# Loading every fourth K of an attention block by transposing DMAs instead of transposing it on TensorE

## The chip, the cores and the metric

The kernel runs on one core of a Trainium2 chip. The metric is the device time of one execution in microseconds (us). A macro step, the unit in which the kernel's work is counted below, takes a few of them.

Names of the engines: PE is TensorE (PEld its weight loads), DVE VectorE, ACT ScalarE, POOL GpSimd, SP SyncE, whose queue issues the loads.

## What is computed

Two attention blocks, A and B, of the same shape are computed one after the other, and their results are put side by side. In each there are 16 batches, 32 heads, 64 queries, 512 cached keys and a head size of 128; all data are bf16.

```python
B, Sq, D = 16, 64, 640
H, Sk, Dh = 32, 512, 128
q = (x @ wq).reshape(B, Sq, H, Dh).transpose(0, 2, 1, 3)
scores = jnp.einsum("bhqd,bhkd->bhqk", q, k_cache) * (Dh ** -0.5)
p = softmax(scores, axis=-1)
o = jnp.einsum("bhqk,bhkd->bhqd", p, v_cache)
out = o.transpose(0, 2, 1, 3).reshape(B, Sq, H * Dh) @ wo
```

K and V are the bulk: 2 blocks x 16 x 32 x 512 x 128 elements of each, 268 MB together, each read once.

## The kernel before

**Tiling.** A step is one head of a pair of batches, whose 64 queries each fill the 128 partitions. Two steps (two heads) are a macro step m; there are 256. Eight macro steps are a group (16 heads of a pair of batches). Eight groups (all 16 batches) are a pass, for one half of a block's heads; there are four passes. The sums of the first half stay in `outp`, and the second half's are added to them.

**One macro step** goes through these operations, each named by two letters or three in the code:

- KX (PE, L433): 8 transposes of 128 x 128 blocks of K into one PSUM bank, for batch j = 0 and again for j = 1. KE (DVE, L442) evicts each to `ktp_ring`.
- QP2 (PE, L451): the projection of q; QE2 (ACT, L459) evicts it to `qT_ring`.
- SM2 (PE, L467): the scores, four matmuls of 512 columns, into one PSUM bank for each head.
- MX (DVE, L476) finds the row maxima, EX (ACT, L482) makes the exponentials and their sums, RC2 (DVE, L488) the reciprocals, NM (POOL, L496) scales each head's rows from `p_ring` into `pn_ring`.
- TR2 (PE, L505): 8 transposes of the scaled rows; TE2 (DVE, L512) evicts them to `pT_ring`.
- PV2 (PE, L524): the product with V; OE2 (ACT, L532) evicts it.
- OP2 (PE, L540 and L545): the product with wo, summed in PSUM over the group. At its end OVP (ACT) or OVF (DVE, L560) takes the sum out, and after OVF a store sends it away.
- For each group XT (PE, L604) and XE (ACT, L612) transpose the next x.

**Order.** The order on each engine is fixed by hand: a template lists the operations of one slot with the offset of the macro step that each belongs to. Engines run their lists in order and wait for each other by semaphores.

```python
PE_T = (("TR2", 1), ("QP2", 4), ("KX", 4, 0), ("SM2", 3), ("PV2", 1), ("XT", 0), ("OP2", 0), ("KX", 4, 1))
ACT_T = (("QE2", 4), ("OE2", 1), ("XE", 0), ("EX", 3, 0), ("EX", 3, 1), ("OV", 0), ("ST", -1))
DVE_T = (("TE2", 1), ("RC2", 2), ("KE", 4, 0), ("MX", 3, 0), ("MX", 3, 1), ("KE", 4, 1), ("OVF", 0))
POOL_T = (("NM", 0, 0), ("NM", 0, 1))
```

In slot k, PE thus transposes the scaled rows of macro step k+1, transposes K for k+4 and makes the scores of k+3. POOL has NM alone, in order.

**Loads.** K and V come in chunks of four heads, 512 KB for each batch, into rings of `NKB` = 5 and `NVB` = 5 chunks. K is laid out so that partition p holds 8 keys of one head in one run of 2,048 bytes (`(p t) d`, t = 8), V so that it holds 4 keys in runs of 1,024 bytes. After KX and KE, the scores' columns therefore stand in another order of the keys, and NM puts them into the order that V has. wq and wo are loaded in quarters of a pass, two passes deep. All loads go through SP's queue, in one order that a planner makes out of the slot in which each is needed, the slot in which its buffer is free, and a table of durations (`DMA_NS`, for 8 heads of a batch in the case of K and V, against `SLOT_NS` = 3600 for a slot). An issue whose buffer isn't free stops all that stand behind it.

Of the kernel before, what the change touches and what calls it, by code (L numbers as in the profile page):

```python
# [14 lines left out]
class Cfg:  # L15
    G = 4
    HH = 16
    NKB = 5
    NVB = 5
    NX = 2  # L20
# [14 lines left out]
    SLOT_NS = 3600.0  # L35
    DMA_NS = dict(LDK=3100.0, LDV=3100.0, LDWQ=3900.0, LDWO=4300.0, LDX=700.0)


class Op:
# [3 lines left out]
    def __init__(self, eng, kind, idx, reads=(), writes=(), dur=0.0, ts=None, aux=None):  # L43
        self.eng = eng
        self.kind = kind
        self.idx = idx
        self.reads = tuple(reads)
        self.writes = tuple(writes)
        self.sem = None
        self.count = None  # L50
        self.deps = []
        self.waits = []
        self.dur = dur
        self.ts = ts
        self.aux = aux
        self.dma = kind in ("LDK", "LDV", "LDX", "LDWQ", "LDWO", "ST")

# [7 lines left out]
def build_plan(dims, cfg):  # L65
# [19 lines left out]
    def step_info(g):  # L85
        grp = g // SPB
        return grp // NBP, grp % NBP, grp, g % SPB
# [7 lines left out]
    for t in cfg.PE_T:  # L95
        OFF.setdefault(t[0], t[1])

    def make_op(kind, m, sub):
        g0, g1 = 2 * m, 2 * m + 1
        ps_, bp, grp, h0 = step_info(g0)  # L100
        c = g0 // G
# [28 lines left out]
        if kind == "SM2":  # L130
            return mk("pe", "SM2", m, [("qT", m % cfg.NQ), ("ktp", m % cfg.NKT, 0), ("ktp", m % cfg.NKT, 1)],
                      [("SB", 0), ("SB", 1)], "SM2", m)
# [80 lines left out]
    def chunk_pieces(c):  # L213
# [5 lines left out]
        return [(0, 0, 0, G), (0, 1, 0, G)]  # L219

    for c in range(NCHUNK):
        m0 = MPC * c
        for kind, ring, n_ring, cons, tb in (("LDK", "kn", cfg.NKB, "KX", 2), ("LDV", "v", cfg.NVB, "PV2", 2.5)):
            ready = NEG if c < n_ring else MPC * (c - n_ring + 1) - 1 - OFF[cons]
            for pi, (piece, j, hlo, hhi) in enumerate(chunk_pieces(c)):
                op = mk("sp", kind, (c, j, piece), [], [(ring, c % n_ring, gi) for gi in range(hlo, hhi)], kind,
                        m0, aux=(c, j, hlo, hhi, piece), dur=cfg.DMA_NS[kind] * (hhi - hlo) / 8.0)
                loads.append((ready, m0 - OFF[cons] + 0.01 * hlo, tb + 0.001 * pi, op))
# [14 lines left out]

    def sem_key(op):
        if op.kind in ("LDK", "LDV"):
            return ("d_" + op.kind[2:].lower(), op.writes[0][1], op.aux[4])
        if op.kind == "LDX":
            return ("d_x", op.writes[0][1])
        if op.kind in ("LDWQ", "LDWO"):
            return ("d_" + op.kind[2:].lower(), op.aux[0] % 2, op.aux[1])  # L250
        if op.kind == "ST":
            return ("d_out", op.aux % 2)
        if op.kind in ("INIT1", "INIT2"):
            return ("s_init",)
        return ("s_" + op.kind.lower(),)
# [91 lines left out]
def mha_kernel(nc, blocks, out, cfg=None):  # L347
# [17 lines left out]
    HH = SPB  # L365
    NKB, NVB, NX, NXN, NQ, NKT, NP, NPN, NT, NO, NR = (cfg.NKB, cfg.NVB, cfg.NX, cfg.NXN, cfg.NQ, cfg.NKT, cfg.NP,
                                                       cfg.NPN, cfg.NT, cfg.NO, cfg.NR)
# [10 lines left out]
    with contextlib.ExitStack() as es:  # L378
        block = es.enter_context(nc.Block())

        def sb(name, shape, dt):
            return es.enter_context(nc.sbuf_tensor(name, shape, dt))
# [6 lines left out]
        kn_ring = sb("kn_ring", [128, NKB, 2, G // 2, 8, DH], BF16)  # L389
        v_ring = sb("v_ring", [128, NVB, 2, G, 4, DH], BF16)  # L390
        ktp_ring = sb("ktp_ring", [128, NKT, 2, 2, SK], BF16)
        qT_ring = sb("qT_ring", [128, NQ, 2, 128], BF16)
# [64 lines left out]
        def em_QE2(e, op):  # L457
            m = op.idx
            ins = e.activation(qT_ring[:, m % NQ].rearrange("p s q -> p (s q)"), q_ps, ACTF.Copy, scale=scale)  # L459
            return ins, ins  # L460

        def em_SM2(e, op):
            m = op.idx
            first = last = None
            for sub in range(2):
                for j in range(2):
                    ins = e.matmul(s_bank(sub)[64 * j:64 * j + 64, :], qT_ring[:, m % NQ, sub, 64 * j:64 * j + 64],  # L467
                                   ktp_ring[:, m % NKT, sub, j, :], start=True, stop=True, tile_position=(0, 64 * j))
                    first = first or ins
                    last = ins  # L470
            return first, last
# [19 lines left out]
        def em_NM(e, op):  # L491
            g = op.idx
            r = g % NR
            src = p_ring[:, g % NP, :].rearrange("q (th tl pp) -> q th tl pp", th=2, tl=4)
            dst = pn_ring[:, g % NPN, :].rearrange("q (tl pp th) -> q th tl pp", tl=4, th=2)
            ins = e.tensor_scalar(dst, src, recip[:, r:r + 1], 1.0, ALU.mult, ALU.mult)  # L496
            return ins, ins
# [112 lines left out]
        def em_XE(e, op):  # L610
# [3 lines left out]
            return ins, ins  # L614

        def em_LDKV(e, op):
            c, j, hlo, hhi, _piece = op.aux
# [5 lines left out]
            else:  # L623
# [7 lines left out]
                        OVP=em_OVP, OVF=em_OVF, ST=em_ST, XT=em_XT, XE=em_XE, INIT1=em_INIT1, INIT2=em_INIT2,  # L631
                        LDWQ=em_LDWQ, LDWO=em_LDWO, LDX=em_LDX, LDK=em_LDKV, LDV=em_LDKV)

# [86 lines left out]
```

## Time and profile before

| | |
|---|---|
| median of 3 runs | 959.31 us (958.41 to 959.53) |
| profiled execution, span | 956.8 us; no other time of it is on the page |
| PE busy | 919.4 us, 96% of the span |
| DVE busy | 841.9 us, 88% |
| ACT, POOL busy | 567.1 us (59%), 416.9 us (44%) |
| granted TensorE clock | 0.998 |
| moved by DMA | 299.5 MB, mean 313 GB/s |
| KX, L433 | 4,096 matmuls, 314.6 us busy |
| KE, L442 | 512 copies, 353.7 us busy |
| NM, L496 | 512 operations of 843 ns |

The span reaches from the first to the last instruction of the core. Busy times of matmuls overlap, since they are pipelined: eight transposes are 0.61 us long in the timeline while the next group starts 0.45 us after them. What PE spends on a group is better read from start to start.

In a line of a timeline stand the start in us from the span's start, the length, the engine, the line of the kernel, the operation, what it writes and reads, the shapes, the count of merged instructions and, in brackets, how long the engine sat idle before and who ended that. In a line of waits stand who waited for whom, the total in us, how often, and the longest.

### The profile page before, as it was taken

To read this page: it belongs to the slowest core of one execution; us is meant where nothing else is said; L and a number is where in the kernel's file an instruction comes from. 1 tells how busy PE (TensorE), PEld (TensorE's weight loads), DVE (VectorE), ACT (ScalarE), POOL (GpSimd) and SP (SyncE) were. 2 spreads that over 40 slices of the span, in tenths; PEclk is the share of its full clock that TensorE was granted. 3 is DMA by queue.
4 is the path that set the end of the run, shared out by engine and by line. 5 is a ranking of instruction groups with operands and counts; after the bars stand their busy time and mean duration, and the time that the engine had idled before them with its cause. 6 is when DMAs were issued, how large, how long until landed. Compare 5 with 4: busy or idle time off the path is not lost.

```text
span 956.8 us, 34351 instructions
## 1 busy us (share of the span) xinstructions
PE 919.4 (96%) x14755; PEld 733.5 (77%) x15008; DVE 841.9 (88%) x1552; ACT 567.1 (59%) x1585; POOL 416.9 (44%) x518
## 2 busy tenths in 40 slices
PE   4999999999999999999999999999999999999997
PEld 3877777778777777877777787777877778777775
DVE  2898899898899999899999899889899998999996
ACT  1666656666665565656566666666666656565654
POOL 0444444444444444444444444444444444444443
PEclk9999999999999999999999999999999999999999
DMA  9999999999999999888999999988888988899830
GB/s 315 364 365 364 351 365 367 365 368 351 338 337 337 343 330 315 299 292 305 322 332 352 326 353 327 306 294 296 302 305 288 308 301 297 295 297 314 295 124 15
DMA packets 230871, 299.51 MB, mean 313 GB/s; under 512 B 9536, under 2 KB 165184, under 8 KB 230720
## 3 DMA queue, kind: packets, MB, share of 16 engines
q1 hardware_dynamic: 228416, 294.69, 91.0%
q8 instruction: 118, 1.93, 0.8%
q10 hardware_dynamic: 2304, 2.62, 0.8%
q14 instruction: 33, 0.27, 0.1%
HBM read 294.65 MB, written 2.62 MB: 311 GB/s over the span
## 4 chain that ended last, share of the span: by engine, by line
PE 89%; DVE 4%; POOL 3%; issue 2%; SPq 1%; DMA 1%; POOLq 0%; DVEq 0%
PE ps L433 22%; PE ps L524 14%; PE ps L451 14%; PE ps L467 14%; PE ps L505 12%; PE ps L545 7%; PE ps L540 5%; POOL pn_ring L496 3%; DVE out_sb L560 1%; DVE ktp_ring L442 1%; DVE pT_ring L512 1%; PE ps L604 1%; DMA xn_ring<-in_A_x_dram 1%; SPq L626 1%; SPq L583 1%
## 5 line engine op out<-in xcount | busy, mean ns | idle before, releaser
L496 POOL TENSOR_SCALAR pn_ring<-p_ring,recip 128x512 bf16<-128x512 bf16 x512 | 416.3, 843 | 532.7 <-DVE recip L488 532.7
L442 DVE COPY ktp_ring<-ps 128x1024 bf16<-128x1024 bf16 x512 | 353.7, 691 | 105.3 <-PE ps L433 85.1
L482 ACT ACTIVATE p_ring<-ps,negmax 128x512 bf16<-128x512 f32 x512 | 345.6, 684 | 4.8 <-DVE negmax L476 4.8
L476 DVE TENSOR_REDUCE negmax<-ps 128x1 f32<-128x512 f32 x512 | 327.3, 681 | 0.4 <-PE ps L467 0.3
L433 PE MATMUL ps<-ident,kn_ring 128*128 128x128 bf16 x4096 | 314.6, 220 | 2.8 <-DMA kn_ring<-in_A_k_cache_dram 1.6
L532 ACT ACTIVATE oT_ring<-ps 128x256 bf16<-128x256 f32 x256 | 98.0, 383 | 306.0 <-PE ps L524 306.0
L433 PEld LDWEIGHTS ps<-ident,kn_ring 128*128 128x128 bf16 x4096 | 251.9, 98 | 34.2 <-DVE ktp_ring L442 2.6
L524 PEld LDWEIGHTS ps<-pT_ring,v_ring 128*128 128x128 bf16 x4096 | 133.5, 98 | 109.2 <-issue 100.0
L451 PE MATMUL ps<-xT_ring,wq_sb 128*128 128x128 bf16 x2560 | 186.4, 220 | 3.2 <-DMA wq_sb<-in_A_wq_dram 3.2
L512 DVE COPY pT_ring<-ps 128x1024 bf16<-128x1024 bf16 x256 | 174.5, 682 | 4.6 <-PE ps L505 3.8
L524 PE MATMUL ps<-pT_ring,v_ring 128*128 128x64 bf16 x4096 | 163.8, 194 | 3.3 <-issue 1.7
L467 PE MATMUL ps<-ktp_ring,qT_ring 128*64 128x512 bf16 x1024 | 159.8, 392 | 0.4 <-ACT p_ring L482 0.4
L505 PE MATMUL ps<-ident,pn_ring 128*128 128x128 bf16 x2048 | 156.7, 219 | 3.5 <-POOL pn_ring L496 3.5
L451 PEld LDWEIGHTS ps<-xT_ring,wq_sb 128*128 128x128 bf16 x2560 | 155.2, 98 | 3.5 <-DMA wq_sb<-in_A_wq_dram 3.5
L459 ACT ACTIVATE qT_ring<-ps 128x256 bf16<-128x256 f32 x256 | 98.4, 384 | 66.8 <-PE ps L451 66.8
L505 PEld LDWEIGHTS ps<-ident,pn_ring 128*128 128x128 bf16 x2048 | 124.1, 98 | 7.0 <-POOL pn_ring L496 6.7
L545 PE MATMUL ps<-wo_sb,oT_ring 128*128 128x128 bf16 x512 | 112.1, 219 | 13.4
L482 ACT ACTIVATION_READ_ACCUMULATOR p_ring<-ps,negmax 128x1 f32 x512 | 105.0, 205 | 0.0
L540 PE MATMUL ps<-wo_sb,oT_ring 128*128 128x512 bf16 x259 | 97.8, 379 | 0.0
L540 PEld LDWEIGHTS ps<-wo_sb,oT_ring 128*128 128x128 bf16 x512 | 50.1, 98 | 30.6 <-ACT oT_ring L532 0.3
L467 PEld LDWEIGHTS ps<-ktp_ring,qT_ring 128*64 128x64 bf16 x1024 | 36.1, 108 | 27.1 <-ACT p_ring L482 0.6
L545 PEld LDWEIGHTS ps<-wo_sb,oT_ring 128*128 128x128 bf16 x512 | 50.1, 98 | 0.0
(13 smaller groups left out, 112.7 us busy)
## 6 DMA issues: line engine op xcount, KB each, us to landing
kn_ring<-in_A_k_cache_dram SPq DMA_DIRECT2D x128, 512.0 KB, 7.0
v_ring<-in_A_v_cache_dram SPq DMA_DIRECT2D x128, 512.0 KB, 7.2
kn_ring<-in_B_k_cache_dram SPq DMA_DIRECT2D x126, 512.0 KB, 4.8
v_ring<-in_B_v_cache_dram SPq DMA_DIRECT2D x126, 512.0 KB, 5.7
wq_sb<-in_A_wq_dram SPq DMA_DIRECT2D x8, 640.0 KB, 10.4
wo_sb<-in_A_wo_dram SPq DMA_DIRECT2D x8, 640.0 KB, 10.2
wq_sb<-in_B_wq_dram SPq DMA_DIRECT2D x8, 640.0 KB, 8.4
wo_sb<-in_B_wo_dram SPq DMA_DIRECT2D x8, 640.0 KB, 7.5
```

Of the source, the lines that this page charges most:

```text
L433: ins = e.transpose(kt_ps[:, t8, :], kn_ring[:, c % NKB, j, hp, t8, :], ident[:, :])
L442: ins = e.tensor_copy(dst, src)
L451: ins = e.matmul(q_ps[:, sub * 128:(sub + 1) * 128], wq_sb[:, ps_ % 2, kt, hh * DH:(hh + 1) * DH], xT_ring[:, grp % NX, kt, :], start=(kt ...
L467: ins = e.matmul(s_bank(sub)[64 * j:64 * j + 64, :], qT_ring[:, m % NQ, sub, 64 * j:64 * j + 64], ktp_ring[:, m % NKT, sub, j, :], start=T ...
L476: ins = e.reduce_max(negmax[:, r:r + 1], s_bank(g % 2), axis=AX.X, negate=True)
L482: ins = e.activation(p_ring[:, g % NP, :], s_bank(g % 2), ACTF.Exp, bias=negmax[:, r:r + 1], scale=1.0, accum_out=rowsum[:, r:r + 1])
L496: ins = e.tensor_scalar(dst, src, recip[:, r:r + 1], 1.0, ALU.mult, ALU.mult)
L505: ins = e.transpose(pt_ps[:, sub, t, :], pn_ring[:, g % NPN, t * 128:(t + 1) * 128], ident[:, :])
L512: ins = e.tensor_copy(pT_ring[:, m % NT].rearrange("p s t q -> p (s t q)"), pt_ps_flat)
L524: ins = e.matmul(o_ps[:, col:col + 64], v_ring[:, c % NVB, j, gi, t, :], pT_ring[:, m % NT, sub, t, 64 * j:64 * j + 64], start=(t == 0), s ...
L540: ins = e.matmul(out_ps0, oT_ring[:, m % NO, sub, :], wo_sb[:, ps_ % 2, hh, 0:N0], start=(hh == 0), stop=(hh == SPB - 1))
L545: last = e.matmul(out_ps1, oT_ring[:, m % NO, sub, :], wo_sb[:, ps_ % 2, hh, N0:DN], start=(hh == 0), stop=(hh == SPB - 1))
```

## The change

In every macro step with m % 4 == 3 (`DEVERY` = 4), K is loaded by two DMAs, one for each batch, that transpose on their way (`LDKT`). Their source is the 2 x 512 rows of two heads, 256 bytes each, in natural key order; their destination is a new ring `kd_ring` of `NKD` = 2 macro steps, from which SM2 reads. These macro steps have no KX and no KE. The plain K load of a chunk that ends in such a macro step is shortened by two heads. NM of these macro steps reads with a step of four elements and writes densely, to go from the natural key order to that of V. `NKB` goes from 5 to 4, and the planner's table gets a duration for the new loads.

```diff
-    NKB = 5
+    NKB = 4
+    NKD = 2
+    DEVERY = 4
...
-    DMA_NS = dict(LDK=3100.0, LDV=3100.0, LDWQ=3900.0, LDWO=4300.0, LDX=700.0)
+    DMA_NS = dict(LDK=3100.0, LDKT=2200.0, LDV=3100.0, LDWQ=3900.0, LDWO=4300.0, LDX=700.0)
...
+    def by_dma(m):
+        return m % cfg.DEVERY == cfg.DEVERY - 1
+
     def make_op(kind, m, sub):
         g0, g1 = 2 * m, 2 * m + 1
+        if kind in ("KX", "KE") and by_dma(m):
+            return None
...
+    for m in range(NMAC):
+        if by_dma(m):
+            i = m // cfg.DEVERY
+            ready = NEG if i < cfg.NKD else m - cfg.NKD * cfg.DEVERY - OFF["SM2"]
+            for j in range(2):
+                op = mk("sp", "LDKT", (m, j), [], [("kd", i % cfg.NKD)], "LDK", m, aux=(m, j), dur=cfg.DMA_NS["LDKT"])
+                loads.append((ready, m - OFF["SM2"] - 1.5, 2 + 0.001 * j, op))
...
+                if kind == "LDK":
+                    while hhi > hlo and by_dma((c * G + hhi) // 2 - 1):
+                        hhi -= 2
+                    if hhi == hlo:
+                        continue
...
+        kd_ring = sb("kd_ring", [128, NKD, 2, 2, SK], BF16)
...
                     ins = e.matmul(s_bank(sub)[64 * j:64 * j + 64, :], qT_ring[:, m % NQ, sub, 64 * j:64 * j + 64],
-                                   ktp_ring[:, m % NKT, sub, j, :], start=True, stop=True, tile_position=(0, 64 * j))
+                                   (kd_ring[:, (m // cfg.DEVERY) % NKD, j, sub, :] if by_dma(m)
+                                    else ktp_ring[:, m % NKT, sub, j, :]), start=True, stop=True, tile_position=(0, 64 * j))
...
             src = p_ring[:, g % NP, :].rearrange("q (th tl pp) -> q th tl pp", th=2, tl=4)
             dst = pn_ring[:, g % NPN, :].rearrange("q (tl pp th) -> q th tl pp", tl=4, th=2)
+            if by_dma(g // 2):
+                src = p_ring[:, g % NP, :].rearrange("q (p t) -> q t p", t=4)
+                dst = pn_ring[:, g % NPN, :].rearrange("q (t p) -> q t p", t=4)
...
+        def em_LDKT(e, op):
+            m, j = op.aux
+            blk, bp, grp, ps_, hh0 = step_info(2 * m)
+            h0 = (ps_ % NHALF) * HH + hh0
+            src = blocks[blk][1][2 * bp + j, h0:h0 + 2].rearrange("h s d -> (h s) d")
+            ins = e.dma_start_transpose(kd_ring[:, (m // cfg.DEVERY) % NKD, j, :, :].rearrange("p h s -> p (h s)"), src)
+            return ins, ins
```

More of the change, by code (lines that the diff above doesn't have):

```diff
@@ L55, in __init__ @@
         self.aux = aux
-        self.dma = kind in ("LDK", "LDV", "LDX", "LDWQ", "LDWO", "ST")
+        self.dma = kind in ("LDK", "LDKT", "LDV", "LDX", "LDWQ", "LDWO", "ST")
 STAGES = ("LDW", "LDX", "LDK", "LDV", "KX0", "KE0", "KX1", "KE1", "QP2", "QE2", "SM2", "MX0", "MX1", "EX0", "EX1",
@@ L130, in make_op @@
         if kind == "SM2":
-            return mk("pe", "SM2", m, [("qT", m % cfg.NQ), ("ktp", m % cfg.NKT, 0), ("ktp", m % cfg.NKT, 1)],
+            kt = [("kd", (m // cfg.DEVERY) % cfg.NKD)] if by_dma(m) else [("ktp", m % cfg.NKT, 0),
+                                                                         ("ktp", m % cfg.NKT, 1)]
+            return mk("pe", "SM2", m, [("qT", m % cfg.NQ)] + kt,
                       [("SB", 0), ("SB", 1)], "SM2", m)
@@ L244, in sem_key @@
     def sem_key(op):
+        if op.kind == "LDKT":
+            return ("d_kd", op.writes[0][1])
         if op.kind in ("LDK", "LDV"):
@@ L365, in mha_kernel @@
     HH = SPB
-    NKB, NVB, NX, NXN, NQ, NKT, NP, NPN, NT, NO, NR = (cfg.NKB, cfg.NVB, cfg.NX, cfg.NXN, cfg.NQ, cfg.NKT, cfg.NP,
+    NKB, NKD, NVB, NX, NXN, NQ, NKT, NP, NPN, NT, NO, NR = (cfg.NKB, cfg.NKD, cfg.NVB, cfg.NX, cfg.NXN, cfg.NQ, cfg.NKT, cfg.NP,
                                                        cfg.NPN, cfg.NT, cfg.NO, cfg.NR)
@@ L460, in em_QE2, with by_dma @@
             return ins, ins
+        def by_dma(m):
+            return m % cfg.DEVERY == cfg.DEVERY - 1
         def em_SM2(e, op):
@@ L631, in mha_kernel @@
                         OVP=em_OVP, OVF=em_OVF, ST=em_ST, XT=em_XT, XE=em_XE, INIT1=em_INIT1, INIT2=em_INIT2,
-                        LDWQ=em_LDWQ, LDWO=em_LDWO, LDX=em_LDX, LDK=em_LDKV, LDV=em_LDKV)
+                        LDWQ=em_LDWQ, LDWO=em_LDWO, LDX=em_LDX, LDK=em_LDKV, LDKT=em_LDKT, LDV=em_LDKV)
         def run_program(e, prog, final_waits=()):
```

## The prediction

> **What bounds the kernel now.** The page first, for which engine is full. The columns of part 1 are busy time, share of the span and number of instructions; part 2 cuts the span in 40 slices (tenths busy, then GB/s).
>
> ```profile
> PE 919.4 (96%) x14755; PEld 733.5 (77%) x15008; DVE 841.9 (88%) x1552; ACT 567.1 (59%) x1585; POOL 416.9 (44%) x518
> ...
> DMA  9999999999999999888999999988888988899830
> GB/s 315 364 365 364 351 365 367 365 368 351 338 337 337 343 330 315 299 292 305 322 332 352 326 353 327 306 294 296 302 305 288 308 301 297 295 297 314 295 124 15
> ```
>
> PE is full, but so nearly are the DMA engines. For the first nine slices they move about 364 GB/s; later the rate falls to 290 to 305. The queue of SP tells why:
>
> ```profile
> SPq L626 <- PE ps L433: 353.5, 119, 4.0
> SPq L622 <- PE ps L524: 123.4, 81, 2.6
> ```
>
> SP stood 477 us (of 956.8) waiting until PE had freed a K or V buffer. So the late rate is the demand of PE, and 364 GB/s is what the loads reach when nothing holds them.
>
> Then one macro step of the steady part, from the timeline (start, us, engine, line):
>
> ```profile
> 801.05 0.61 PE L505 MATMUL ps<-ident,pn_ring 128*128 128x128 bf16 x8
> 801.26 0.69 DVE L442 COPY ktp_ring<-ps 128x1024 bf16<-128x1024 bf16 x1 [0.23 <-PE ps L433]
> 801.86 0.68 DVE L512 COPY pT_ring<-ps 128x1024 bf16<-128x1024 bf16 x1
> 802.06 0.61 PE L433 MATMUL ps<-ident,kn_ring 128*128 128x128 bf16 x8
> 802.46 0.15 DVE L488 RECIPROCAL recip<-rowsum 128x2 f32<-128x2 f32 x1
> 802.60 0.62 PE L467 MATMUL ps<-ktp_ring,qT_ring 128*64 128x512 bf16 x4
> 802.71 1.63 POOL L496 TENSOR_SCALAR pn_ring<-p_ring,recip 128x512 bf16<-128x512 bf16 x2 [1.95 <-DVE recip L488]
> 804.17 0.61 PE L433 MATMUL ps<-ident,kn_ring 128*128 128x128 bf16 x8
> 804.62 0.55 PE L505 MATMUL ps<-ident,pn_ring 128*128 128x128 bf16 x7
> ```
>
> The reader is to see two loops that close in the same slot. PE's own work runs from TR2 (L505) at 801.05 to the next TR2 at 804.62: 3.57 us with no gap. Beside it runs a chain: TR2, then on DVE the second K eviction (L442), TE2 (L512), RC2 (L488), on POOL the two NM (L496) until 804.34, then the next TR2. It has only 0.28 us to spare. Where OVF (L560) is put into DVE's part of it, it does set the end:
>
> ```profile
> 812.03 0.61 PE L505 MATMUL ps<-ident,pn_ring 128*128 128x128 bf16 x8
> ...
> 812.85 0.81 DVE L560 TENSOR_TENSOR out_sb<-ps,outp 128x640 bf16<-128x640 f32 x1
> ...
> 814.42 1.62 POOL L496 TENSOR_SCALAR pn_ring<-p_ring,recip 128x512 bf16<-128x512 bf16 x2 [2.68 <-DVE recip L488]
> ...
> 816.10 0.62 PE L505 MATMUL ps<-ident,pn_ring 128*128 128x128 bf16 x8 [0.15 <-POOL pn_ring L496]
> ```
>
> NM ends at 816.04 and TR2 starts at 816.10, so the hop is 0.06 us; this slot lasts 4.07 us.
>
> **What the change takes from the compute engines.** 64 of 256 macro steps (m = 3, 7, ...) lose both KX and both KE. By the starts on PE the first KX takes 0.54 us (802.06 to 802.60) and the second 0.45 (804.17 to 804.62): 0.99 us, 63 us in all. DVE loses 2 x 0.69 us in the same slot, 88 us in all. But these all leave one slot, k = m - 4, and the other three keep their 3.57 us. In the shortened slot PE needs 2.58 us, while the chain still stands: the K eviction at its head belongs to the slot before. TR2 to NM's end 3.29 us, plus the hop, 3.35. So PE waits about 0.77 us for NM, and the slot gains 3.57 - 3.35 = 0.22 us: 14 us for 64. The following slot gains nothing, being bound by PE.
>
> One more gain: OVF falls at k = 7, 15, ..., which are slots that lose their KX. There it can run while PE waits for NM, and the slot after starts without the K eviction. The 0.50 us that it costs 16 times (4.07 - 3.57) go: 8 us. The compute engines thus ask for 956.8 - 22 = 935 us of span.
>
> NM of these macro steps reads its source with a step of 4 elements and writes densely, where it now reads densely and writes with a step of 2 (0.843 us each). Nothing shows the new form; from half to double the time gives two-sided bounds of -0.8 and +1.7 us a macro step against a cover of 0.28, so at worst 64 x 1.4 = 90 us on the 935, and no gain if shorter, because those slots are bound by PE. I take no change, the same 512 elements on the same engine being the only row. The Trainium skill (GPSIMD Engine Reference, section on performance pitfalls for Q7 kernels) puts a step in price, about half as much again, where step times element size exceeds 8 bytes; here it is exactly 8, so it would say no change, and this trace shows no such case.
>
> The K ring goes from 5 chunks to 4. A load is then ready 7 macro steps ahead of its KX, 25 us, where the longest K load took 11.0 us to land: nothing. Smaller K loads and an SM2 that reads kd_ring cost nothing on PE, the shapes being the same.
>
> **What it puts on the DMA engines.** This decides. Before: 294.65 MB read and 2.62 written. 64 x 2 loads of 262,144 bytes, 33.6 MB, leave the plain ones: 263.7 MB in all, at 364 GB/s 724 us. What loads at the start fell short by (315 against 364 over 23.9 us) adds 3 us. Behind the last load some work remains; the last KX started at 943.8 of 956.8, and with V landing after K I take 10 of those 13 us. So if the transfers bind, span = 737 + 128 T, with T the time in which the sixteen engines pass one transposing load of 256 KB. It equals 956.8 at T = 1.72 us, and 935 at T = 1.55.
>
> T is not in the trace. Its packets give the bounds. The records have a median of 84 ns for 2,048 bytes, 46 for 1,024, 9 for the 4-byte counts at the end of a load.
> - Below: as now, 8 packets of 2,048 bytes for each engine: 0.67 us. The same bytes are moved, so no less.
> - If only the reading side counts: 84 and 46 ns lie on 8 ns plus 38 for each KB, so a row of 256 bytes takes 17.5 ns; 1,024 rows on 16 engines are 64 each, 1.12 us.
> - Above: each source row is 128 elements that go to 128 partitions. If it is written in 32-byte pieces at 8 + 1.2 ns, 64 x 8 pieces take 4.7 us.
>
> The middle of 1.12 and 4.7 in ratio is 2.3 us. The planner table that is in the diff has 2.2 us. Its other entries stand close to this trace (1.55 us for 512 KB of K, where 364 GB/s gives 1.44), so scaled alike it gives 2.05. I take 2.05, which lies between the two packet rows and a little under their middle. Then 737 + 128 x 2.05 = 999 us of span, and every slot waits for loads, so the 22 us of compute gain are not seen. The end of the program outside the span was 2.5 us (median 959.31 against this execution's 956.8; the page has no other time for it): 1002 us.
>
> The Trainium skill speaks both ways. DMA: Bandwidth & Descriptors, section on latency and other measured facts, has a transposing load at 261 GB/s, which makes an estimated T of 1.0 us and a span of 935. VectorE: DVE Perf Modes, section on the three transpose paths, has 1309 ns for one 128 x 128 block by DMA; eight of them in a row would be an estimated 10.5 us and a span near 2080. No run here shows either.
>
> SP issues 10 loads of K and V in four macro steps, two of them transposing, and waits in order. A load's issue took 0.37 us when free, up to 3.1 when the queue was full. Two at 3.1 and eight at 0.5 are 10 us of 14: hidden. What is behind a transposing load on SP's queue and in the rings (plain K, V, weights) comes later by T, and that is in the sum.
>
> **The rivals.**
> - *Faster, transfers hidden.* T under 1.55 us, as the 17.5 ns row would have it. For it: it is the nearest packet row, and SP's 477 us of waiting are room. Span 935, with some 2 us lost at the start where transfers are short: 937 to 940 with the 2.5.
> - *PE takes the whole gain.* 956.8 - 63 = 894, reported 896. Against it: the 0.28 us of slack of the NM chain, and the slots with OVF that wait for it already. 2 in 100.
> - *Much slower.* The writing side prices the row in small pieces: T = 4.7 makes 737 + 602 = 1339 us. It begins, for this count, at T = 2.6 (1070).
> - *Between.* T from 1.68 to 1.75: transfers just balance what the compute engines gain, about 959.
>
> **How the numbers follow.** A change below about 0.2% can't be told from none here. Forecast (T from 1.75 to 2.6, 963 to 1073 us) 0.43; transfers hidden or nearly (T under 1.68) 0.37 and whole gain 0.02: faster 0.39; between: same 0.04; much slower 0.14. So slower is 0.57. The range for 8 in 10 takes the hidden case, the balance and the forecast, 934 to 1073, and leaves out 0.14 above and 0.03 below. The forecast's own range is 963 to 1073.
>
> **What would show it.** Right: SP's waits for PE at L626 and L622 nearly gone; DMA at 9 in all slices; PE waiting at L433, L467 or L524 for kn_ring, kd_ring or v_ring; T, as the time added for 128 loads beyond 737 us, near 2. In any case L433 shows 3,072 matmuls and L442 384 copies. Wrong: SP still waits for hundreds of us, PE's idle time stands before L505 and is released by pn_ring, some 0.8 us in every fourth slot, and the slots with OVF are 3.57 us long: then T was under 1.55 and the chain through NM sets the time.

## The result and the profile after

The changed kernel takes 1013.34 us, the median of 4 runs (1005.94 to 1014.99), against 958.86 us (957.75 to 959.53, 4 runs) for the kernel before on the same chip. The ratio is 1.0555, with a 95% interval from 1.0519 to 1.0591: slower by 5.6%. The profiled execution took 1014.99 us; its span is 1013.2 us, and the granted TensorE clock in it was 0.983, against 0.998 before. In the changed kernel KX is L458, KE L467, SM2 L495, RC2 L517, NM L528, TR2 L537, PV2 L556 and OVF L592; the K loads are issued at L666, the V loads at L662, the transposing loads at L653.

From the page: the busy times, the DMA rows of the 40 slices, and the packet count.

```profile
PE 905.0 (89%) x13984; PEld 682.4 (67%) x13984; DVE 768.5 (76%) x1424; ACT 565.5 (56%) x1585; POOL 404.9 (40%) x518
...
DMA  9999999999999999999999999999999999999996
GB/s 289 308 285 286 306 284 288 296 318 282 317 309 288 300 296 311 287 304 291 305 322 300 313 305 279 274 320 287 297 319 279 319 292 318 303 290 289 313 306 145
DMA packets 349615, 299.40 MB, mean 295 GB/s; under 512 B 144672, under 2 KB 300320, under 8 KB 349472
```

No compute engine is at its limit any more: PE falls from 96% of the span to 89%, DVE from 88% to 76%. The DMA engines are full to the last slice. Yet they move less than before: the first nine slices, most of them at about 364 GB/s before, are at 284 to 318, and no slice reaches more than 322. Packets under 512 bytes are 144,672 where they were 9,536; 131,072 of them are the 256-byte packets of the transposing loads.

From the waits (who waited for whom, total us, times, longest), the lines of PE in which a load or NM is waited for:

```profile
PE ps L537 <- POOL pn_ring L528: 18.8, 48, 0.6
PE ps L458 <- DMA kn_ring<-in_B_k_cache_dram: 17.5, 19, 2.8
PE ps L458 <- DMA kn_ring<-in_A_k_cache_dram: 17.4, 19, 4.6
PE ps L556 <- DMA v_ring<-in_B_v_cache_dram: 14.3, 12, 3.1
PE ps L556 <- DMA v_ring<-in_A_v_cache_dram: 13.8, 10, 3.9
```

PE now stands for K and V, 63 us in these four lines; with the smaller lines of x, wq and wo it is 78 us, where the kernel before had 12 (x, wq and the first K). The list has no wait for `kd_ring` itself: PE waits for the plain loads that are queued around the transposing ones. This is 65 us more than before, out of the 78 us between the span and the 935 us that the compute engines ask for; what share of the other 13 the lower clock has is not told apart.

The queue of SP, its waits and then a stretch of its timeline (start, us, engine, line, operation, tiles, number of issues merged):

```profile
SPq L653 <- PE ps L495: 124.4, 52, 5.3
SPq L666 <- PE ps L458: 53.0, 57, 2.5
```

```profile
644.58 2.48 SPq L666 DMA_DIRECT2D kn_ring<-in_B_k_cache_dram  x2
647.11 8.00 SPq L653 DMA_TRANSPOSE kd_ring<-in_B_k_cache_dram  x2
655.16 2.85 SPq L662 DMA_DIRECT2D v_ring<-in_B_v_cache_dram  x2
658.05 1.04 SPq L666 DMA_DIRECT2D kn_ring<-in_B_k_cache_dram  x2
```

The list of waits has 177 us of the 477. The timeline says that even this is too much: each issue begins some 0.05 us after the one before it has ended. Added up over the trace, SP is in the middle of an issue for 963 of 1013 us, and only 2 us lie in pauses above 0.1 us. Before, it was 412 us, and the pauses were 489. (Issues don't count as busy, so the view can name PE for time that was spent issuing. Below, "pauses" are counted in this way.) SP no longer waits for buffers. It is held inside its own issues, the longest being the two transposing ones with 8 us.

Last, one shortened slot, from the timeline of PE and POOL:

```profile
603.86 0.61 PE L537 MATMUL ps<-ident,pn_ring 128*128 128x128 bf16 x8
...
605.51 1.62 POOL L528 TENSOR_SCALAR pn_ring<-p_ring,recip 128x512 bf16<-128x512 bf16 x2 [1.94 <-DVE recip L517]
...
607.19 0.62 PE L537 MATMUL ps<-ident,pn_ring 128*128 128x128 bf16 x8 [0.50 <-POOL pn_ring L528]
```

TR2 to TR2 is 3.33 us, and what PE waits for is NM. The predicted slot was 3.35 us. The slot that follows it, with KX in it again, should last 3.57 us; over the run it has a mean of 4.41 and a median of 4.12. The shortened slots keep a median of 3.34, so the waits for loads fall behind each pair of transposing loads and not in every slot.

### The profile page after: what moved, and what is told of

Same layout as the page of the kernel before. It is cut to its first block, busy times and chain, and to the rows that moved or that the text cites. A ratio compares the mean times of both kernels' runs of the same rounds, so it can differ in the third digit from the quotient of the medians.

```text
span 1013.2 us, 32630 instructions
## 1 busy us (share of the span) xinstructions
PE 905.0 (89%) x13984; PEld 682.4 (67%) x13984; DVE 768.5 (76%) x1424; ACT 565.5 (56%) x1585; POOL 404.9 (40%) x518
## 2 busy tenths in 40 slices
DMA packets 349615, 299.40 MB, mean 295 GB/s; under 512 B 144672, under 2 KB 300320, under 8 KB 349472
## 3 DMA queue, kind: packets, MB, share of 16 engines
HBM read 261.10 MB, written 2.62 MB: 260 GB/s over the span
## 4 chain that ended last, share of the span: by engine, by line
PE 44%; DMA 28%; SPq 18%; POOL 4%; DVE 3%; ACT 2%; issue 1%; POOLq 0%; DVEq 0%
DMA kn_ring<-in_B_k_cache_dram 12%; SPq L653 12%; PE ps L458 11%; DMA kn_ring<-in_A_k_cache_dram 11%; PE ps L495 8%; PE ps L556 7%; PE ps L476 6%; PE ps L572 5%; PE ps L537 5%; POOL pn_ring L528 4%; SPq L662 3%; SPq L666 2%; DVE ktp_ring L467 2%; DVE pT_ring L544 1%; PE ps L577 1%
## 5 line engine op out<-in xcount | busy, mean ns | idle before, releaser
L528 POOL TENSOR_SCALAR pn_ring<-p_ring,recip 128x512 bf16<-128x512 bf16 x512 | 404.2, 815 | 601.1 <-DVE recip L517 601.1
L467 DVE COPY ktp_ring<-ps 128x1024 bf16<-128x1024 bf16 x384 | 265.7, 692 | 148.7 <-PE ps L458 137.6
L458 PE MATMUL ps<-ident,kn_ring 128*128 128x128 bf16 x3072 | 238.6, 221 | 36.8 <-DMA kn_ring<-in_B_k_cache_dram 17.5
L458 PEld LDWEIGHTS ps<-ident,kn_ring 128*128 128x128 bf16 x3072 | 189.2, 99 | 68.3 <-DMA kn_ring<-in_B_k_cache_dram 20.9
L556 PEld LDWEIGHTS ps<-pT_ring,v_ring 128*128 128x128 bf16 x4096 | 136.0, 99 | 139.1 <-issue 92.1
L556 PE MATMUL ps<-pT_ring,v_ring 128*128 128x64 bf16 x4096 | 166.6, 195 | 29.8 <-DMA v_ring<-in_B_v_cache_dram 14.3
L537 PE MATMUL ps<-ident,pn_ring 128*128 128x128 bf16 x2048 | 158.5, 221 | 18.9 <-POOL pn_ring L528 18.8
L572 PE MATMUL ps<-wo_sb,oT_ring 128*128 128x512 bf16 x512 | 169.5, 385 | 3.2 <-DMA wo_sb<-in_B_wo_dram 3.2
L537 PEld LDWEIGHTS ps<-ident,pn_ring 128*128 128x128 bf16 x2048 | 124.0, 99 | 37.8 <-POOL pn_ring L528 35.8
L495 PE MATMUL ps<-ktp_ring,qT_ring 128*64 128x512 bf16 x768 | 120.2, 393 | 4.1
L495 PEld LDWEIGHTS ps<-ktp_ring,qT_ring 128*64 128x64 bf16 x768 | 27.1, 108 | 26.4 <-ACT p_ring L511 9.3
```

The lines of the kernel that those rows point to most:

```text
L458: ins = e.transpose(kt_ps[:, t8, :], kn_ring[:, c % NKB, j, hp, t8, :], ident[:, :])
L467: ins = e.tensor_copy(dst, src)
L537: ins = e.transpose(pt_ps[:, sub, t, :], pn_ring[:, g % NPN, t * 128:(t + 1) * 128], ident[:, :])
L556: ins = e.matmul(o_ps[:, col:col + 64], v_ring[:, c % NVB, j, gi, t, :], pT_ring[:, m % NT, sub, t, 64 * j:64 * j + 64], start=(t == 0), s ...
L572: ins = e.matmul(out_ps0, oT_ring[:, m % NO, sub, :], wo_sb[:, ps_ % 2, hh, 0:N0], start=(hh == 0), stop=(hh == SPB - 1))
```

## The experiments

The theories, with the letters that the expectations use. A: what the transposing loads cost is time on the DMA engines that belongs to transposing. B: what binds is SP, held for 3.9 us by each transposing issue. C: the cost is that of 256-byte rows, transposed or not. Later came Q: the loss is made in SP's queue, by small packets that stand in a row. All runs were timed against the kernel before in three rounds; ratios are against that, with the 95% interval. "Span" is that of the profiled execution.

### Rows of 256 bytes, not transposed

The same bytes in the same 256-byte source rows go by a plain DMA into the same ring. The scores of these macro steps are then made from K that is not transposed.

```diff
-            ins = e.dma_start_transpose(kd_ring[:, (m // cfg.DEVERY) % NKD, j, :, :].rearrange("p h s -> p (h s)"), src)
+            dst = kd_ring[:, (m // cfg.DEVERY) % NKD, j, :, :].rearrange("p h (r d) -> p (h r) d", d=DH)
+            ins = e.dma_start(dst, src.rearrange("(r p) d -> p r d", p=128))
```

> The 128 loads into kd_ring move the same 256 KB in rows of 256 bytes, but do not transpose (the scores of these macro steps are made from K that is not transposed). Theory A (a transposing load holds the sixteen DMA engines about 2.06 us, 1.15 us of it in 64 packets of 18 ns and the rest standing in one long packet) and theory B (SP needs 3.9 us to issue one, 8 us for a pair, and the engines run dry meanwhile) both expect that the loads are hidden: T = 1.15 us, 737 + 128 x 1.15 = 884 us of transfers, under the 935 of the compute engines; about 937 us, with SP waiting for PE for more than 200 us. Rival C, that small packets by themselves are the cost, expects 1000 us or more. If the compute engines' part of the prediction is wrong and PE takes its whole gain, 896.

Measured: 969.95 us (965.82 to 973.33), ratio 1.0114 (1.0081 to 1.0148), span 971.6. It lies between, and each theory missed: 43 us of the slowdown need the transposing, but without it the change still loses 11 us, where the compute engines alone would allow about 937. SP is in the middle of an issue for 915 of the 972 us, with 2 us of pauses.

### Rows of 2,048 bytes, not transposed

The same load with 2,048-byte rows, which is what the plain K loads have, again not transposed.

```diff
+            dst = kd_ring[:, (m // cfg.DEVERY) % NKD, j, :, :].rearrange("p h s -> p (h s)")
+            ins = e.dma_start(dst, src.rearrange("(p r) d -> p (r d)", p=128))
```

> The 128 loads into kd_ring move the same 256 KB without transposing, in rows of 2,048 bytes as the other K loads (the scores of these macro steps are made from K that is not transposed). If the size of the rows is what held the run with 256-byte rows at 970 us, this one is bound by the compute engines, as the run with V loaded once was: 944 to 948 us. If the shorter K ring or the order of SP's queue costs something, it stays between 955 and 975.

Measured: 938.03 us (937.36 to 939.23), ratio 0.9789 (0.9774 to 0.9803), span 937.5. The rate in slices and the waits of SP:

```profile
GB/s 313 365 368 366 335 289 309 314 293 322 364 366 369 330 309 317 309 291 332 347 366 369 357 307 322 292 291 322 290 359 365 368 357 318 302 314 317 294 241 16
```

```profile
SPq L667 <- PE ps L458: 174.2, 91, 3.3
SPq L654 <- PE ps L495: 172.5, 52, 4.5
```

With large rows the slices reach 364 GB/s again, SP waits for buffers again, and the whole compute gain appears. Rings, order, extra issues and the new NM therefore cost next to nothing (one early slot of 9.7 us is all that stands out, and runs with the change have one of 9 to 11 us as well); the loss lies in how `kd_ring` is filled.

### V loaded once

Loads of V beyond the first five chunks are left out and the old V is used again, so that transfers can't bind.

```diff
             for pi, (piece, j, hlo, hhi) in enumerate(chunk_pieces(c)):
+                if kind == "LDV" and c >= cfg.NVB:
+                    continue
```

> V is loaded only for the first five chunks and used again after that, so 125 MB of plain loads are gone; the transposing loads stay as they are and stand almost alone in the queue. All theories expect the compute engines' bound, about 935 us of span and 937 us. The trace then shows a transposing load without a full queue ahead of it: theory A expects that the engines still stand in one long packet of about 1 us for each load, theory B that the issue on SP still takes about 3 us or more although nothing is queued; if the issue was long only because the queue was full, it falls to about 0.5 us. The slots without K transposes should be 3.35 us long and the slots with OVF 3.57.

Measured: 944.31 us (943.12 to 945.55), ratio 0.9849 (0.9834 to 0.9864), span 943.0. From the page, the waits of SP and the tile view (issue in ns, shortest/median/longest):

```profile
DMA  9999956556987565556697556557466556556540
```

```profile
SPq L655 <- PE ps L497: 256.9, 62, 4.5
SPq L668 <- PE ps L460: 215.8, 115, 2.9
```

```profile
L655 SPq DMA_TRANSPOSE kd_ring<-in_A_k_cache_dram x64: 1160/1304/5857, 6.4 to 451.5; - x64
```

The DMA engines are half idle. The shortened slots last 3.33 to 3.35 us, those with OVF 3.58, and 7 of the 8 us above 935 are one early slot of 10.8 us. And a transposing issue takes 1.30 us here, where SP pauses for 514 us, not 3.9: the other 2.6 us in the changed kernel don't belong to the issue itself, and a full queue is the nearest reading. That speaks against B. The sign that was expected of A is there in part: 6.5 packets of more than 0.4 us for each transposing load, against 14 in the change.

### The two transposing loads apart

```diff
-                loads.append((ready, m - OFF["SM2"] - 1.5, 2 + 0.001 * j, op))
+                loads.append((ready, m - OFF["SM2"] - 3.5 + 2.0 * j, 2 + 0.001 * j, op))
```

> The load for the first batch of each pair is placed two macro steps earlier in SP's order, so that plain loads stand between the two transposing ones. Theory B expects a large gain: a single issue of 3.9 us is covered by the 5 us of loads that are queued ahead, so the engines no longer run dry; 940 to 965 us. Theory A expects no change, 1005 to 1018 us, since each load holds the engines as long as before.

Measured: 1019.93 us (1018.96 to 1020.86), ratio 1.0634 (1.0617 to 1.0652), 7 us more than the change. If SP's stretch of 8 us had been the trouble, two shorter ones (a median of 3.0 us for an issue) would have helped. B's gain did not come; A, too, had expected no more than 1018.

### V issued by ACT

From the sixth chunk on V is issued from ACT's queue at the end of a slot, and SP issues K, x and the weights alone.

```diff
+            if eng == "act" and k % MPC == 0 and cfg.NVB <= k // MPC + cfg.NVB < NCHUNK:
+                c = k // MPC + cfg.NVB
+                for piece, j, hlo, hhi in chunk_pieces(c):
+                    progs["act"].append(mk("act", "LDV", (c, j, piece), [],
+                                           [("v", c % cfg.NVB, gi) for gi in range(hlo, hhi)], "LDV", MPC * c,
+                                           aux=(c, j, hlo, hhi, piece)))
...
+                if kind == "LDV" and c >= n_ring:
+                    continue
```

> From the sixth chunk on, V is loaded from ACT's queue (two issues of 0.4 us in every second macro step), K and the transposing loads stay with SP. Theory B expects that V fills the time in which SP issues the transposing loads, and that SP's list gets about 180 us shorter: 940 to 965 us. Theory A expects 1005 us or more, since the sixteen engines are full whoever issues, and ACT may be held when the queue is full.

Measured: 1082.31 us (1081.78 to 1091.37), ratio 1.1311 (1.1265 to 1.1356). The waits of SP:

```profile
SPq L662 <- PE ps L504: 322.1, 59, 9.1
```

This total is not standing: counted as above, SP is in the middle of an issue for 1027 of the 1080 us, and its pauses are 9 us. SP's list has lost 178 us of V issues and takes longer all the same, because a transposing issue now takes a median of 4.8 us. So its length is no fixed price of SP's, which is a second sign against B, though the gain that B expected had no fair test with a second queue beside it. ACT's 248 issues of V take a median of 0.49 us (at most 2.8), and PE waits for K above all, 88.7 us in two lines. Why two queues on the same DMA engines cost 69 us is not shown.

### Each transposing load twice

Each is issued again, into the half of `kn_ring` that the shortened K loads leave unused.

```diff
-            for j in range(2):
+            for j in range(4):
...
-            m, j = op.aux
+            m, jc = op.aux
+            j = jc % 2
+            dst = kd_ring[:, (m // cfg.DEVERY) % NKD, j, :, :].rearrange("p h s -> p (h s)")
+            if jc >= 2:
+                dst = kn_ring[:, (m // 2) % NKB, j, 1, :, :].rearrange("p t d -> p (t d)")
...
+            ins = e.dma_start_transpose(dst, src)
```

> Every transposing load is issued a second time into a part of kn_ring that nobody reads, all four of a macro step in a row, so that the time added for 128 loads is the cost of a transposing load while the transfers bind. If each has a cost of its own of 2.06 us, as the plain transfers lost in the changed kernel say: 1013 + 264 = 1277 us. If the engines wait for each other only at the first of a row and later ones cost their packets, 128 x 1.15 = 147 us more: 1160.

Measured: 1198.58 us (1196.10 to 1201.71), ratio 1.2508 (1.2478 to 1.2538). 128 more loads add 185.2 us, so one more transposing load, behind the pair that is there, costs 1.45 us while transfers bind. (The granted clock was 0.921 here and 0.955 in the next run; SP pauses for 2 us in each, as in the change, so the transfers set the time and the clock is not counted.) That is less than the 2.16 us which the prediction's own formula gives for the change, (1013.2 - 737) / 128, and more than its packets alone.

### Each plain 256-byte load twice

The same edit on the plain 256-byte loads.

> The run with plain 256-byte rows, each such load issued twice (the second copy is not read, the first is not transposed). If a load of 256-byte rows costs its 64 packets of 18 ns: 970 + 128 x 1.15 = 1117 us. If it costs what the first 128 seem to by my sum, (971.6 - 737)/128 = 1.83 us: 1204. The difference to the transposing loads issued twice is what the transposing itself costs.

Measured: 1108.46 us (1107.39 to 1118.08), ratio 1.1593 (1.1535 to 1.1651). 138.5 us for 128 loads: 1.08 us each. The packet records have a median of 18 ns for a 256-byte packet, and 64 of those for each engine are 1.15 us. So of the 1.45 us, 1.08 are the rows and 0.37 the transposing; the difference between the change and its plain twin comes to much the same, 43.4 / 128 = 0.34.

### Each transposing load in two halves

```diff
-            for j in range(2):
+            for j in range(4):
...
+            m, jh = op.aux
+            j, h = jh // 2, jh % 2
+            ins = e.dma_start_transpose(kd_ring[:, (m // cfg.DEVERY) % NKD, j, h, :], blocks[blk][1][2 * bp + j, h0 + h])
```

> Each transposing load is cut in two of 512 rows, four in a row for a macro step. If the sixteen engines wait for each other once for every load (about 0.9 us over the packets), 128 more of them add 116 us: 1130. If they wait once for each row of loads, or if the cost goes with the rows: 1005 to 1025.

Measured: 1027.32 us (1025.03 to 1035.06), ratio 1.0733 (1.0689 to 1.0778). 14 us for 128 more loads, 0.11 us each: the cost goes mainly with the rows or bytes, not with the number of loads.

### Transposing with source rows of 2,048 bytes

```diff
-            src = blocks[blk][1][2 * bp + j, h0:h0 + 2].rearrange("h s d -> (h s) d")
+            src = blocks[blk][1][2 * bp + j, h0:h0 + 2].rearrange("h (p t) d -> (h p) (t d)", t=8)
+            dst = kd_ring[:, (m // cfg.DEVERY) % NKD, j].rearrange("p h s -> p (h s)").rearrange("p (t r) -> p t r", t=8)
+            ins = e.dma_start_transpose(dst, src)
```

SM2 then reads `kd_ring` in the key order of the plain loads, and NM keeps its old form everywhere.

> The transposing loads take source rows of 2,048 bytes (8 keys of a partition of the plain layout in a row, 128 rows); the scores read kd_ring with a step, and NM keeps its old form. If a transposing load makes its packets of whole source rows, the queue holds eight packets for an engine instead of 64 and T falls below 1.2 us: 938 to 950 us. If each row is cut to pieces of 256 bytes anyway, 1,024 packets a load remain and the time with them: 1005 to 1020.

Measured: 1007.79 us (1005.93 to 1012.30), ratio 1.0520 (1.0494 to 1.0547). The packets, from the page:

```profile
DMA packets 349615, 299.40 MB, mean 298 GB/s; under 512 B 144672, under 2 KB 300320, under 8 KB 349472
```

They are the same to the last one as in the change: a transposing load goes in packets of 256 bytes with source rows of 256 and of 2,048 bytes. Long rows don't help: the 5.5 us to the change lie within the scatter of the two (1005.93 to 1012.30 against 1005.94 to 1014.99).

### Plain 256-byte rows, spread over four macro steps

Back to the plain twin, whose 970 us are too much for what its packets cost: the plain bytes at 364 GB/s with the prediction's 13 us for start and end make 737, and 128 x 1.08 add 138, so 875, well under the 937 of the compute engines. The trace says what happens around a pair. Take the loads that are issued and not yet landed when a long issue (over 1.5 us) ends, and count them whole, per engine: the median is 128 packets in the kernel before, 144 in the change and 168 in the plain twin. In the change 8 of 10 of these counts lie between 136 and 156 packets, though they come from 3 to 6 loads and 48 to 186 KB. So what the queue holds goes by packets rather than by loads or bytes, some 130 to 170 in this count; in the plain twin it scatters from 112 to 208, so a fixed number is a reading of it and not shown. With large rows so many packets are many microseconds of transfers. Two loads of 64 rows of 256 bytes fill most of it with 32 KB for each engine; they are gone in some 2.3 us, and SP, held until there is room, has little that is large queued behind them. In the plain twin the packets in flight then fall from 17 to 10 on 16 engines for about a microsecond (mean of the 64 pairs). This is theory Q, and it can be tried: the same small rows as four loads of half the size, apart from each other among the large ones.

```diff
-            for j in range(2):
-                op = mk("sp", "LDKT", (m, j), [], [("kd", i % cfg.NKD)], "LDK", m, aux=(m, j), dur=cfg.DMA_NS["LDKT"])
-                loads.append((ready, m - OFF["SM2"] - 1.5, 2 + 0.001 * j, op))
+            for j in range(4):
+                op = mk("sp", "LDKT", (m, j), [], [("kd", i % cfg.NKD)], "LDK", m, aux=(m, j), dur=cfg.DMA_NS["LDKT"] / 2)
+                loads.append((ready, m - OFF["SM2"] - 4.5 + j, 2 + 0.001 * j, op))
...
+            dst = kd_ring[:, (m // cfg.DEVERY) % NKD, j, h, :].rearrange("p (r d) -> p r d", d=DH)
+            ins = e.dma_start(dst, blocks[blk][1][2 * bp + j, h0 + h].rearrange("(r p) d -> p r d", p=128))
```

> Plain loads with 256-byte rows as in the run that took 970 us (no transposing), but in four loads of 512 rows for a macro step, spread one macro step apart in SP's order, so that the queue never holds more than 32 small packets of an engine between two large loads. Theory Q (SP's queue holds some 130 packets for each engine whatever their size; two loads of 64 small packets push the large loads out of it, and the engines run dry behind them) expects 938 to 950 us. If small packets simply cost their time, or if the engines are full in any order: 965 to 975.

Measured: 958.75 us (957.11 to 962.00, 10 runs), ratio 1.0002 (0.9992 to 1.0012). The waits of SP:

```profile
SPq L654 <- PE ps L495: 130.1, 41, 5.0
```

Between the two again, but SP now really stands (132 us of pauses, by the count above): the first of the four loads is due 4.5 macro steps ahead, before SM2 has freed its buffer, and holds up what is queued behind it. The same edit with the need one macro step later:

```diff
-                loads.append((ready, m - OFF["SM2"] - 4.5 + j, 2 + 0.001 * j, op))
+                loads.append((ready, m - OFF["SM2"] - 3.5 + j, 2 + 0.001 * j, op))
```

> As the spread 256-byte loads before, which took 959 us, but each of the four placed one macro step later in SP's order. In that run SP stood 132 us before these loads, waiting for kd_ring to come free, with the large loads held behind them. If those waits were what was left over, and theory Q is right for the rest (small packets in a row push the large loads out of the queue), it comes near the compute engines' bound: 938 to 948 us, with SP's waits at these loads well under 100 us. If the engines are simply that much slower at 256-byte packets: 955 to 962 again.

Measured: 942.77 us (942.02 to 943.32), ratio 0.9832 (0.9815 to 0.9848), span 941.6.

```profile
SPq L654 <- PE ps L495: 110.4, 34, 5.4
SPq L667 <- PE ps L458: 31.6, 37, 2.0
```

The same bytes in the same 256-byte packets, and more loads, take 27 us less than in pairs. Ten or fewer packets are in flight for 77 us of the plain twin, 60 of the first spread and 34 of this one (from 50 us on to the last issue). That is what Q forecast for plain small rows, and the order alone is worth the 16 us between the two spread runs; four halves in a row were not tried with plain loads. The waits of SP didn't fall as expected, 110 us for 130: it still stands for `kd_ring`, and why that costs so much less time now is not shown.

### Every eighth macro step

Half as many transposing loads, in the macro steps whose shortened slot is the one that holds OVF.

```diff
-    DEVERY = 4
+    DEVERY = 8
...
-        return m % cfg.DEVERY == cfg.DEVERY - 1
+        return m % cfg.DEVERY == 3
```

> Only every eighth macro step (m = 3, 11, ...) loads its K by transposing DMAs, those whose slot also has OVF. The compute engines then gain 32 x 0.22 + 16 x 0.50 = 15 us: 942 us of span, 3 us more at the start. Transfers: 280.5 MB of plain loads at 364 GB/s are 771 us, with 13 for start and end and 64 x 2.16 = 138 for the transposing loads 922, so they hide. 944 to 948 us. If the loss from transposing loads comes by the row and not on the average, with K or V late after each of them, 955 or more.

Measured: 949.07 us (948.84 to 950.16), ratio 0.9903 (0.9888 to 0.9918), span 948.4. From the waits of SP and the timeline of PE:

```profile
SPq L666 <- PE ps L458: 191.8, 81, 5.2
```

```profile
603.61 0.61 PE L537 MATMUL ps<-ident,pn_ring 128*128 128x128 bf16 x8
606.94 0.62 PE L537 MATMUL ps<-ident,pn_ring 128*128 128x128 bf16 x8 [0.29 <-POOL pn_ring L528]
610.52 0.61 PE L537 MATMUL ps<-ident,pn_ring 128*128 128x128 bf16 x8
```

This kernel leaves nothing out and beats both kernels, by 9.7 and 64 us. Half the loads leave SP waiting for PE again, so transfers are hidden (PE stands 16 us for loads, before 12, the change 78). The slot lasts 3.33 us and the next 3.58. Since the OVF slots are among the shortened ones, the part of the compute gain that they carry is kept whole: by the prediction's terms 8 + 32 x 0.22 = 15 of the 22 us are on offer. 9.7 came; one slot near the start lasts 10.8 us, as with V loaded once, and takes 7 of them back, while the first TR2 starts 1.4 us earlier than before.

## Why the prediction was right, point by point

**The forecast held**: 1002 us against 1013.34, slower, with every slice of the DMA row at 9 (the last at 6), PE standing for K and V, and SP's pauses gone. (1013.2 - 737) / 128 = 2.16 us is the T of its formula, against 2.05. Not every slot waits for loads, as it had it: the shortened ones keep a median of 3.34 us, and the loss stands behind the pairs. The 2.5 us outside the span, taken from two different executions, are 1.7 to 1.8 in the runs. The rivals didn't come: neither hidden transfers, nor the whole of PE's gain, nor a balance, and on the other side the T of the formula stayed under the 2.6 us from which the much slower case was counted.

**The compute gain** was right and is shown: 3.33 us for a slot predicted at 3.35, 3.58 for the OVF slots predicted at 3.57 (V loaded once). Where transfers are out of the way the kernel takes 938.03 us, in the 937 to 940 of the hidden rival (2,048-byte rows). PE's 63 us of removed work was worth 21 (958.59 to 938.03) where 22 were forecast, because NM's chain bounds the shortened slot.

**NM's new form** was taken at no change. It is somewhat shorter, a median of 728 ns for the 128 of the new form against 844 for the old in the same execution, and it gains nothing, those slots being bound by PE.

**The K ring at four chunks** at nothing: right, the 2,048-byte run has it too. The counts of L458 and L467 are the predicted ones:

```profile
L467 DVE COPY ktp_ring<-ps 128x1024 bf16<-128x1024 bf16 x384 | 265.7, 692 | 148.7 <-PE ps L458 137.6
...
L458 PE MATMUL ps<-ident,kn_ring 128*128 128x128 bf16 x3072 | 238.6, 221 | 36.8 <-DMA kn_ring<-in_B_k_cache_dram 17.5
```

**SP's issue** was the prediction's weak point. It allowed 0.37 to 3.1 us for an issue and called the sum hidden, 10 us of 14 for four macro steps. It was 15.0 of 15.8 us (963 and 1013 over 64). A transposing issue takes 1.2 to 1.3 us with room in the queue and 3.9 in the change, so the longer sum follows from a full queue and is not what sets the time, as far as the runs against B go; but what keeps the queue full so long is something that the sum didn't contain.

**The term 737 + 128 T** came out near, and by luck: no row of the trace had T, and the 2.05 us are the planner's table scaled, between a lower bound of 1.12 and an upper one of 4.7. The lower one was nearly exact for plain rows (18 ns a packet against 17.5, and 1.08 us a load by loads twice). The upper one supposed pieces of 32 bytes, and no run shows any. A transposing load behind others costs 1.45 us, 0.37 more than the plain one. With 1.45 the formula gives 737 + 186 = 923 us, under the 935 of the compute engines, so with the better price of one more load the forecast would have been the hidden case, and wrong. What is left over is 1013.2 - 186 = 828 us, 91 more than the 737, which assumed that the plain loads keep 364 GB/s as long as nothing holds them. For the plain twin the same count gives 969.95 less 1.7 us outside the span and less 138, 830. There the loss is the neighbours', and of order: at least 27 us of it go when the loads are spread out.

For the transposing loads the packet records put it in another place, in the loads themselves. Their 256-byte packets take 2.41 us for each load and engine in the change, where the plain twin's take 1.38, and 161 of the 309 us that this makes over the run lie in packets of more than 0.4 us, of which plain loads have none. With each load issued twice the records grow by 1.46 us for each added load, as the time did, but by only 30 us in the long packets. So a transposing load behind another is cheaper than one that stands among plain ones, and 1.45 us is not the price of the first. Whether the 2.05 us were a good price of a load in its place, or too much for the load and made good by a loss of its neighbours that was left out, can't be told from these runs. In either case the sum did not contain what makes the load dear.

**What stays open** is what the long packets stand for. The change has about 14 of them in each load, a median of 1.4 us long. In all they take 161 us for each engine in the change, 161 with the loads in halves, 192 with the two of a pair apart and 191 with each load twice: cutting adds none, though it costs 14 us of time, and keeping the loads apart, which helped plain rows, adds 31 (the time rises by 7, to 1019.93). The sixteen engines end a transposing load within 0.2 us of each other at the median, where those of a plain load in the change are 1.4 us apart; with the pair kept apart the plain loads, too, end within 0.1 to 0.2. From 1.0 to 0.5 us before the second issue of a pair ends, all loads together move 37 to 68 GB/s with about 22 packets in flight (mean of the 64 pairs): the engines aren't empty there, they stand. That looks as if each row of transposing loads held all the engines until the last has caught up, but the records don't name the engine that is late, and transposing halves spread over four macro steps weren't tried.

Two statements of the Trainium skill can be set beside this. DMA: Bandwidth & Descriptors, section on latency and other measured facts, gives a transposing load 261 GB/s, measured with a middle dimension that is not contiguous; here, with rows that follow each other in memory, 262,144 bytes in 1.45 us are 181 GB/s for one more load, and in place, by the 2.16 us of the formula, 121 GB/s. The page Advanced Engine Details and Errata, in its section on the X-bar transpose of TRN2, holds that transposing DMAs are as fast as regular ones; here the transposing load costs 0.34 to 0.37 us more than a plain one of the same rows, and 43 us over the kernel.

## What to carry to other kernels

To price a new kind of load, issue it twice where transfers already bind: the slope is what one more costs behind the first. Set it beside what the first ones cost in place; the difference, 0.7 us a load here, is lost in the order of the queue or in engines that stand, and packets in flight and long packets help to tell which. A queue whose room goes by packets holds little time when its packets are small, so plain loads with small rows are better apart from each other, among large ones (27 us here); transposing loads kept apart took 7 us more. An issue that grows longer can be the sign of a full queue. Before an engine is relieved, look in which slots the work falls and what chain is next there: here 63 us off PE were worth 21, and half of the change, in the slots that hold the longest chain, was the part worth having.

## What the runs showed of the hardware that was not expected

- When a long issue on SP ended, the loads not yet landed had 128, 144 and 168 packets for each DMA engine at the median (before, change, plain twin); in the change 8 of 10 counts lay between 136 and 156 packets, but between 48 and 186 KB.
- The 128 transposing loads went in 131,072 packets of 256 bytes with source rows of 256 as with rows of 2,048 bytes.
- The sixteen engines finished a transposing load within 0.2 us of each other at the median, a plain one of the change within 1.4 us; with the two transposing loads of a pair apart, the plain K and V loads, too, finished within 0.1 to 0.2 us.
- In the change 161 us for each DMA engine lay in 256-byte packets of more than 0.4 us, some 14 in each transposing load; plain 256-byte loads had none. With each transposing load twice it was 191 us, in halves 161.
- The page's count of bytes read from HBM leaves the transposing loads out: 261.10 MB in the change, and the same with each of them issued twice, against 294.65 for the plain twin.
- NM with a read step of four elements and dense writes took 728 ns, with dense reads and a write step of two 844 ns.
